# Attention and two feed-forward layers: factors, sums, squares and the mean square take other places in the order

## The chip, the cores and the metric

The kernel runs on one core of a Trainium2 chip. The metric is device microseconds of that core, the median of several runs. Engines are named as in the profile: PE is TensorE (PEld its weight loads), DVE is VectorE, ACT is ScalarE, POOL is GpSimd, SP is SyncE, which only issues DMAs here.

## The reference

Soft-capped attention over 2 batches of 12 heads (448 tokens, head size 64), then a gated feed-forward layer behind an RMS norm, then a second one with a PReLU:

```python
scores = cap * np.tanh(scale * q @ k.T / cap)
attn = np.exp(scores - max); attn = attn / (attn.sum(-1) + 1e-9)
x = (attn @ v)                      # to 896 tokens x 768
xn = x / np.sqrt(np.mean(x * x, -1) + 1e-6) * rms_g
x = silu(xn @ w_gate) * (xn @ w_val) @ w_out      # 768 -> 1536 -> 768
h = x @ w_in                                      # 768 -> 2048
return (np.maximum(h, 0) + alpha * np.minimum(h, 0)) @ w_out2
```

## The kernel before

Heads are worked on in 12 pairs (0 to 11; pairs 0 to 5 are batch 0, 6 to 11 batch 1). The whole order is written by hand. In round `i` of the pair loop TensorE computes the scores of pair `i` (`qk_tail`, L219, and `qk`, three tiles of L229), and then for pair `i - 1` the softmax sums (`sums`, L290, with the tail of the values' product, L272) and the values' product (`pv`, L256). ScalarE makes tanh (L240) and exp (L243) of the scores.

VectorE runs through a list of small steps in each round:

- `evac_o(i - 2)` (L320, tile `ee`) copies a finished product out of PSUM.
- `recip`, in odd rounds (L338 to L343, tiles `gf`, `th`, `tl`), turns the softmax sums of a couple of pairs into factors, cuts them in a high and a low part, and sends both by DMA to `r`. It waits for the DMA that gathers the sums (`gt`, L331).
- `prep(i + 1)` (L195 `hi`, L196 `lo`) cuts the next pair's q and k in two parts.
- `w_bits` (L122, tile `wt`) makes a weight of the feed-forward layer from its packed form: the "remainder" of the title. `w_next` behind it issues the load of another packed weight on SP's queue.
- `evac_u(i - 1)` (L328, tile `us`) copies the softmax sums out of PSUM and issues the two small `gt` DMAs.

In even rounds from 4 on, `norms` spreads the factors of an earlier couple over the partitions on TensorE (L373, `rps`), and VectorE multiplies (L377, `xf`). GpSimd squares those results (`square`, L353 to L361) and adds up the squares of a batch in one tile (`s_546` for batch 0). It also forms sums and differences of weights (`sum1` to `sum4`, L130 `wt<-wt`).

In round 9 `rms_sum` (L398, `ms`) reduces the squares of batch 0 on TensorE, into the PSUM tile with tag "o". That tag has one buffer: the product of a pair (`oo`), the second factor tile of `norms` and `ms` take it in turn, so that each waits until VectorE has read the one before. VectorE copies `ms` out at L572 (tile `spare`).

Behind the last pair, `sums(last)` takes one PSUM tile of two banks, the softmax sums in one (`us`), the product in the other (`oo`). Then the two layers follow as one long chain of block products (L450, L462, L796, L826), in which hooks with a number and a rank put ScalarE's and VectorE's work behind a product. In the first layer's output product, `osplit` and `osplit_low` (L1059, L672, `xx<-b,xx`) make the high and low parts of each operand; "P6" is one of its seven products.

Of the kernel before, what the change touches and what calls it, by code (L numbers as in the profile page):

```python
# [7 lines left out]
F32 = mybir.dt.float32  # L8
# [9 lines left out]
P = 128  # L18
B, H, S, D = 2, 12, 448, 64
# [38 lines left out]
def attn_moe_kernel(ctx: ExitStack, tc: tile.TileContext, units, qk_in, v, sel, w, gvec, alpha, out):  # L58
    nc = tc.nc
# [188 lines left out]
    def upper(name):  # L248
        return ps_o.tile([P, 512], F32, tag="o", name=name)
# [27 lines left out]
    def sums(i):  # L277

        t = pt[i]
        if i == last:  # L280
            both = ps_s.tile([P, 2, 512], F32, tag="s", name="us")
            us[i], oo[i] = both[:, 0], both[:, 1]
        else:
            us[i] = under()
            if i:
                oo[i] = upper("oo")

        def add(h, x, k, m=slice(0, P), src=None):
            q = h + 2 * x
            nc.tensor.matmul(  # L290
                us[i][q * Q:q * Q + Q, HALF[0]], ones[m, :Q], t[m, k, src or HALF[x]], start=k == 2 * TG,
                stop=k // 2 == TG - 1, skip_group_check=True,
            )

        pv_tail(i, False)
        for h in range(2):
            for x in range(2):
                if split[i]:
                    add(h, x, 2 * TG, HEAD[x], HALF[h])
                else:  # L300
                    add(h, x, 2 * TG, HEAD[h])
        if i == 0 and split[i]:
            pv_tail(i, True)
        for n in range(2 * TG):
            for x in range(2):
                add(n % 2, x, n)
        if i and split[i]:
            pv_tail(i, True)
# [58 lines left out]
    def under():  # L367
        return ps_r.tile([P, 512], F32, tag="u", name="rps")
# [10 lines left out]
    def norms(i, *to):  # L379
        for fn in (spread, scaled):  # L380
            for j, rps in enumerate(to):
                fn(i + j, rps)
# [9 lines left out]
    ms_of = {}  # L392

    def rms_sum(b, ms):
        ms_of[b] = ms
        parts = s2.pop(b)
        for n, t in enumerate(parts):
            nc.tensor.matmul(ms[:, :S], ones, t, start=n == 0, stop=n == len(parts) - 1)  # L398

    def rms_keep(b):  # L400
        spare[b] = xpool.tile([P, K3, S], F32, tag="B22h", name="spare")
        rstd[b] = spare[b][:, 2]
# [65 lines left out]
    with tc.manual_schedule():  # L468
# [44 lines left out]
        def a(i, fn, *args):  # L513
            first.setdefault(i, []).append((fn, args))

        def z(i, fn, *args):
            second.setdefault(i, []).append((fn, args))

        conv = conv_seq[:]
        for x in ("A12", "A11"):  # L520
            for g in range(2):
# [4 lines left out]
        for i in range(NPAIR):  # L526
            a(i, load_raw, i + 2)
            a(i, load_v, i + 1)
            if i == 1:
                for put, u in zip((a, z), conv[1:RAW]):  # L530
                    put(i, w_load, u)
            steps = [(prep, i + 1)]
            if i % 2 == 1 and i > 2:
                steps.insert(i < 9, (recip, (i - 3) // 2))
            for step in steps:
                a(i, *step)
            if i - 2 in range(len(conv)):
                a(i, w_bits, conv[i - 2])
                if i - 2 < len(conv) - RAW:
                    a(i, w_next, conv[i - 2])  # L540
            if i % 2 == 0 and i > 2:
                for j in range(2):
                    (a if i == 8 else z)(i, square, i - 4 + j)
            if i - 1 in range(len(conv)):
                if i < 5:
                    z(i, w_top, conv[i - 1], nc.vector.tensor_copy)
                else:
                    a(i, w_top, conv[i - 1])
        a(9, rms_root, 0)
        for n, j in ((3, 0), (4, 1), (9, 6)):  # L550
            z(n, w_hi, conv[j], nc.vector.tensor_copy)
            (a if n == 9 else z)(n + (n == 9), w_lo, conv[j])
        a(11, w_hi, conv[7])
        for put, n, fn, g in ((z, 6, sum1, 0), (z, 7, sum1, 1), (z, 7, sum2, 0), (a, 8, sum2, 1), (a, 8, sum3, 0),
                              (z, 8, sum3, 1), (z, 10, sum4, 0)):
            put(n, fn, "g", g)
        z(10, rms_tail, 0)
# [2 lines left out]
        for i in range(NPAIR):  # L560
            pairs = i % 2 == 0 and i > 2
            if i > 2:
                evac_o(i - 2)
            if i:
                home = {1: (ps_r, "u"), 2: (ps_o, "o")}.get(i)
                qk(i, TG, home[0].tile([P, 1, 512], F32, tag=home[1], name="s") if home else third())
            if i == 8:
                norms(i - 4, under(), upper("rps"))
            if i == 9:
                rms_sum(0, upper("ms"))  # L570
                rms_keep(0)
                nc.vector.tensor_copy(rstd[0], ms_of[0][:, :S])  # L572
                ms_of[0] = rstd[0]
            two = lambda: ps_s.tile([P, 2, 512], F32, tag="s", name="s")
            for g in range(TG - 1):
                qk(i, g, two())
                if pairs and i != 8 and g == 0:
                    norms(i - 4, under(), upper("rps"))
                if (i, g) == (1, 0):
                    oo[0] = upper("oo")  # L580
                    pv(0, range(2))
            if i == 0:
                qk(0, TG - 1, third())
                qk(0, TG, two())
            if i == 1:
                pv(0, range(2, TG))
            if i == 10:
                sums(i - 1)
            if i:
                qk(i, TG - 1, third())  # L590
            soft(i)
            for fn, args in first.pop(i, []):
                fn(*args)
            if i and i != 10:
                sums(i - 1)
            if i == 1:
                evac_o(0)
            if i:
                evac_u(i - 1)
                if i > 1:  # L600
                    pv(i - 1)
                del pt[i - 1], hi[i - 1], lo[i - 1], vt[i - 1]
            for fn, args in second.pop(i, []):
                fn(*args)
# [469 lines left out]

        for way, p, js, hi_at, lo_at in (
# [4 lines left out]
        ):  # L1080
            for h, j in enumerate(js):
                do(o0 + hi_at[h], 0.2, osplit, way, p, j, h)
                do(o0 + lo_at[h], 2.2, osplit_low, way, p, j, h)
        for n, *abc in ((-22, 0, 4, 1, 0), (-21, 0, 5, 3, 4), (-20, 0, 1, 3, 1), (-9, 1, 4, 1, 0), (-8, 1, 5, 3, 4),
                        (-7, 1, 1, 3, 1), (4, 2, 0, 1, 0), (7, 2, 0, 3, 0)):
            do(o0 + n, 3.5, o_sum, *abc)
# [261 lines left out]
```

## Time and profile before

| | us |
|---|---|
| median of 3 runs (539.45 to 539.93) | 539.74 |
| the profiled execution's own time | 540.45 |
| its span | 538.7 |
| TensorE busy in the span | 530.2 (98%) |
| VectorE busy | 448.2 (83%) |
| ScalarE busy | 400.6 (74%) |
| GpSimd busy | 112.0 (21%) |

The chain of work that ended last lies on TensorE for 88% of the span. Times in rows are microseconds from the start of the span. A row of the timeline begins with its start and its duration and ends with the idle time of the engine before it, where there was any, and what ended it.

### The profile page before, as it was taken

The numbers are of one execution on the slowest core, as the hardware profiler recorded it, in microseconds if no ns is written. First come the engines' busy times: TensorE is split into PE (matmuls) and PEld (weight loads), VectorE is DVE, ScalarE is ACT, GpSimd is POOL, SyncE is SP. The second block draws the span as 40 slices with busy tenths as digits, with TensorE's granted clock in tenths as the row PEclk, the third lists the DMA queues.
The fourth block names the chain that finished last, engine by engine and source line by source line (L and its number), as shares of the span: only waits on it lengthen the run. The fifth ranks groups of instructions, "written<-read, shape, count | busy, mean of one in ns | idle before, by whom it ended". The sixth has DMA issues, their size and how long they took to land.

```text
span 538.7 us, 8345 instructions
## 1 busy us (share of the span) xinstructions
PE 530.2 (98%) x3322; PEld 451.1 (84%) x3322; DVE 448.2 (83%) x516; ACT 400.6 (74%) x475; POOL 112.0 (21%) x80
## 2 busy tenths in 40 slices
PE   8999999999999999999999999999999999999997
PEld 5554544699999999999998999999999999999996
DVE  5588889798999968689779796869997897998951
ACT  7989989476766665477688776789989996995530
POOL 0023763300066441010013011110210231210000
PEclk9999999999999999999999999999999999999999
DMA  6856520400344426047865759433466789564111
GB/s 214 317 168 230 179 76 11 159 19 2 102 133 175 161 90 219 0 176 250 273 179 101 157 196 308 80 58 125 169 235 225 215 226 205 98 145 111 51 52 51
DMA packets 22343, 80.05 MB, mean 149 GB/s; under 512 B 3744, under 2 KB 6688, under 8 KB 22304
## 3 DMA queue, kind: packets, MB, share of 16 engines
q1 hardware_dynamic: 16378, 65.43, 35.4%
q0 software_dynamic: 5552, 13.70, 13.9%
q8 instruction: 26, 0.43, 0.3%
q10 hardware_dynamic: 374, 0.39, 0.2%
q14 instruction: 13, 0.11, 0.1%
HBM read 62.99 MB, written 2.75 MB: 122 GB/s over the span
## 4 chain that ended last, share of the span: by engine, by line
PE 88%; DVE 5%; ACT 3%; POOL 2%; DMA 1%; issue 1%; DVEq 0%; SPq 0%; ACTq 0%
PE s L450 19%; PE x L450 13%; PE m L450 13%; PE s L826 8%; PE x L826 7%; PE x L796 5%; PE s L796 5%; PE m L826 4%; PE m L796 3%; PE s L229 2%; PE oo L256 2%; PE rps L290 2%; PE s L462 1%; ACT pt L243 1%; DVE wt L122 1%; PE oo L272 1%
## 5 line engine op out<-in xcount | busy, mean ns | idle before, releaser
L143 DVE TENSOR_TENSOR wl<-wt,wh 128x768 fp32r<-128x768 f32 x109 | 111.5, 1024 | 21.2 <-ACT wh L137 20.8
L137 ACT CAST wh<-wt 128x768 fp32r<-128x768 f32 x106 | 87.7, 830 | 39.7 <-PE s L826 9.2
L130 POOL TENSOR_TENSOR wt<-wt 128x768 f32<-128x768 f32 x25 | 58.4, 2341 | 164.7 <-DVE wl L143 75.7
L117 ACT CAST top<-raw 128x768 f16<-128x768 bf16 x64 | 68.9, 1077 | 21.1 <-DMA raw<-w_in 11.6
L122 DVE SCALAR_TENSOR_TENSOR wt<-raw,top 128x768 uint32<-128x768 uint32 x64 | 66.8, 1045 | 1.0 <-ACT top L117 1.0
L450 PE MATMUL s<-xx,wh 128*128 128x448 f32 x264 | 63.6, 365 | 0.0
L672 DVE TENSOR_TENSOR xx<-b,xx 128x896 fp32r<-128x896 f32 (+1 forms) x55 | 62.1, 1135 | 0.0
L450 PEld LDWEIGHTS s<-xx,wh 128*128 128x128 f32 x264 | 49.3, 187 | 4.8 <-issue 0.9
L450 PE MATMUL x<-xx,wh 128*128 128x448 f32 x204 | 49.9, 366 | 0.0
L450 PE MATMUL m<-xx,wh 128*128 128x448 f32 x204 | 49.5, 364 | 0.0
L893 POOL DMA_DIRECT2D wt<-wt x25 | 21.6, 864 | 126.6 <-DVE wt L122 62.0
L240 ACT ACTIVATE pt<-s,cinv 128x896 f32<-128x896 f32 (+1 forms) x48 | 40.8, 910 | 5.0 <-PE s L229 2.4
L450 PEld LDWEIGHTS x<-xx,wh 128*128 128x128 f32 x204 | 38.2, 188 | 3.5 <-issue 0.4
L450 PEld LDWEIGHTS m<-xx,wh 128*128 128x128 f32 x204 | 38.3, 188 | 3.0
L826 PE MATMUL s<-xx,wh 128*128 128x448 f32 x144 | 40.5, 362 | 0.0
L826 PE MATMUL x<-xx,wh 128*128 128x448 f32 x128 | 36.0, 362 | 0.0
L243 ACT ACTIVATE pt<-pt,cap_t 128x3136 f32<-128x3136 f32 (+2 forms) x13 | 35.2, 2711 | 0.4
L450 PE MATMUL s<-xx,wl 128*128 128x448 f32 x132 | 33.8, 364 | 0.0
L796 PE MATMUL s<-xx,wh 128*128 128x448 f32 x108 | 30.4, 362 | 0.0
L826 PEld LDWEIGHTS s<-xx,wh 128*128 128x128 f32 x144 | 27.0, 187 | 2.3
L796 PE MATMUL x<-xx,wh 128*128 128x448 f32 x96 | 27.3, 363 | 0.6 <-DVE xx L672 0.6
L256 PE MATMUL oo<-pt,vt 128*32 128x448 f32 x264 | 27.1, 540 | 0.4 <-ACT pt L243 0.4
(208 smaller groups left out, 1124.7 us busy)
## 6 DMA issues: line engine op xcount, KB each, us to landing
raw<-w_in SPq DMA_DIRECT2D x68, 768.0 KB
wt<-wt POOLq DMA_DIRECT2D x25, 384.0 KB, 5.3
rw<-qk_in SPq DMA_DIRECT2D x11, 480.0 KB
vt<-v_in SPq DMA_DIRECT2D x12, 288.0 KB
lent<-wt POOLq DMA_DIRECT2D x5, 384.0 KB, 7.0
b<-b POOLq DMA_DIRECT2D x4, 448.0 KB, 5.3
out<-P SPq DMA_DIRECT2D x5, 224.0 KB
out<-b SPq DMA_DIRECT2D x2, 448.0 KB
```

Of the source, the lines that this page charges most:

```text
L117: copy(top_of[u].bitcast(F16)[:, 1::2], raw_t[u].bitcast(BF16)[:, 4:4 * n + 4:4])
L122: nc.vector.scalar_tensor_tensor(out=f_t[u].bitcast(U32), in0=raw_t.pop(u).bitcast(U32)[:, 1:2 * n + 1:2], scalar=13, in1=top_of.pop(u), o ...
L130: add(out=t, in0=f_t[a], in1=f_t[b], op=op)
L137: copy(h_t[u], f_t[u].rearrange("p (k m) -> p k m", m=P))
L143: nc.vector.tensor_tensor(out=l_t[u], in0=f_t[u].rearrange("p (k m) -> p k m", m=P), in1=h_t[u], op=ALU.subtract)
L240: nc.scalar.activation(out=part, in_=st.pop((i, g)), func=AF.Tanh, scale=cinv)
L243: nc.scalar.activation(out=t[:, done:to], in_=t[:, done:to], func=AF.Exp, scale=cap_t)
L256: nc.tensor.matmul(oo[i][q * Q:q * Q + Q, :S], vv[:, n, q % 2 * Q:q % 2 * Q + Q], t[:, n, :], start=i == c == 0, stop=i > 0 and c == TG - ...
L450: nc.tensor.matmul(ps[:, r, :S], lhs, rhs, start=first and n == 0, stop=n == len(mm) - 1, skip_group_check=True,)
L672: nc.vector.tensor_tensor(out=out, in0=a, in1=b, op=op)
L796: nc.tensor.matmul(dst[m], wt[:, kk * MB + m, :], x, start=first and u == 0 and kk == 0 and n == 0, stop=u == UO - 1 and kk == 1 and n == ...
L826: nc.tensor.matmul(dst[m], wt[:, kk * MB + m, :], x, start=first and u == kk == i == 0, stop=last and kk == 1 and i == 2, skip_group_check ...
```

## The change

- `recip` comes ahead of `prep` in rounds 3, 5 and 7 too. (Round 7's `prep` is that of pair 8.)
- In rounds 4, 6 and 8 `sums(i - 1)` and `evac_u(i - 1)` are written ahead of `w_bits`. TensorE's order stays; VectorE's copy and SP's two `gt` DMAs come earlier in their queues.
- `sum2` of weight group 0 goes from behind round 7 to behind the squares of round 8 on GpSimd.
- In round 9 `rms_sum` stands behind the first score tile, and the copy out of PSUM (`keep_sum`) behind `w_bits`.
- The last pair's sums and product get a PSUM tile each.
- The first low part of "P6" is made one hook earlier.

```diff
@@ -278,8 +278,7 @@
         t = pt[i]
         if i == last:
-            both = ps_s.tile([P, 2, 512], F32, tag="s", name="us")
-            us[i], oo[i] = both[:, 0], both[:, 1]
+            us[i], oo[i] = (ps_s.tile([P, 2, 512], F32, tag="s", name=x)[:, 0] for x in ("us", "oo"))
         else:
@@ -516,6 +515,7 @@
+        EARLY = (4, 6, 8)
         conv = conv_seq[:]
@@ -531,10 +531,13 @@
             if i % 2 == 1 and i > 2:
-                steps.insert(i < 9, (recip, (i - 3) // 2))
+                steps.insert(0, (recip, (i - 3) // 2))
             for step in steps:
                 a(i, *step)
             if i - 2 in range(len(conv)):
+                if i in EARLY:
+                    a(i, sums, i - 1)
+                    a(i, evac_u, i - 1)
                 a(i, w_bits, conv[i - 2])
@@ -546,12 +549,19 @@
+
+        def keep_sum():
+            rms_keep(0)
+            nc.vector.tensor_copy(rstd[0], ms_of[0][:, :S])
+            ms_of[0] = rstd[0]
+
+        a(9, keep_sum)
         a(9, rms_root, 0)
...
-        for put, n, fn, g in ((z, 6, sum1, 0), (z, 7, sum1, 1), (z, 7, sum2, 0), (a, 8, sum2, 1), (a, 8, sum3, 0),
+        for put, n, fn, g in ((z, 6, sum1, 0), (z, 7, sum1, 1), (a, 8, sum2, 0), (a, 8, sum2, 1), (a, 8, sum3, 0),
@@ -566,16 +576,13 @@
-            if i == 9:
-                rms_sum(0, upper("ms"))
-                rms_keep(0)
-                nc.vector.tensor_copy(rstd[0], ms_of[0][:, :S])
-                ms_of[0] = rstd[0]
             two = lambda: ps_s.tile([P, 2, 512], F32, tag="s", name="s")
             for g in range(TG - 1):
                 qk(i, g, two())
                 if pairs and i != 8 and g == 0:
                     norms(i - 4, under(), upper("rps"))
+                if (i, g) == (9, 0):
+                    rms_sum(0, upper("ms"))
@@ -591,12 +598,13 @@
-            if i and i != 10:
+            if i and i != 10 and i not in EARLY:
                 sums(i - 1)
...
             if i:
-                evac_u(i - 1)
+                if i not in EARLY:
+                    evac_u(i - 1)
@@ -1074,13 +1082,13 @@
-            (2, "P5", (4, 4, 0), (2, 3, 5), (4, 5, 6)), (0, "P6", (5, 5, 0), (5, 6, 8), (8, 8, 9)),
+            (2, "P5", (4, 4, 0), (2, 3, 5), (4, 5, 6)), (0, "P6", (5, 5, 0), (5, 6, 8), (7, 8, 9)),
...
-                do(o0 + lo_at[h], 2.2, osplit_low, way, p, j, h)
+                do(o0 + lo_at[h], 1.5 if (p, h) == ("P6", 0) else 2.2, osplit_low, way, p, j, h)
```

VectorE in round 9, before; the rows run from the copy of pair 7's product to that of pair 8's softmax sums.

```order
L320 COPY ee<-oo 128x448
L572 COPY spare<-ms 128x448
L338 TENSOR_SCALAR gf<-gt,eps_t 64x28
L339 RECIPROCAL gf<-gf 64x28
L342 CAST th<-gf 64x28
L343 TENSOR_TENSOR tl<-gf,th 64x28
L195 CAST hi<-rw 128x832
L196 TENSOR_TENSOR lo<-rw,hi 128x832
L122 SCALAR_TENSOR_TENSOR wt<-raw,top_94 128x768
L328 COPY us<-rps 128x224
```

The same place now:

```order
L319 COPY ee<-oo 128x448
L337 TENSOR_SCALAR gf<-gt,eps_t 64x28
L338 RECIPROCAL gf<-gf 64x28
L341 CAST th<-gf 64x28
L342 TENSOR_TENSOR tl<-gf,th 64x28
L195 CAST hi<-rw 128x832
L196 TENSOR_TENSOR lo<-rw,hi 128x832
L122 SCALAR_TENSOR_TENSOR wt<-raw,top_94 128x768
L555 COPY spare<-ms 128x448
L327 COPY us<-rps 128x224
```

The copy of `ms` went from the second place to the ninth, behind seven steps that have nothing to do with it.

GpSimd in rounds 7 to 10, before; `wt<-wt` are the weights' sums, `sq` and `s_546` the squares of batch 0, `s_1149` that of batch 1.

```order
L130 TENSOR_TENSOR wt<-wt 128x768 x3
L357 TENSOR_TENSOR sq<-xf 128x448
L361 TENSOR_TENSOR s_546<-s_546,sq 128x448
L357 TENSOR_TENSOR sq<-xf 128x448
L361 TENSOR_TENSOR s_546<-s_546,sq 128x448
L130 TENSOR_TENSOR wt<-wt 128x768 x3
L353 TENSOR_TENSOR s_1149<-xf 128x448
```

The same place now:

```order
L130 TENSOR_TENSOR wt<-wt 128x768 x2
L356 TENSOR_TENSOR sq<-xf 128x448
L360 TENSOR_TENSOR s_546<-s_546,sq 128x448
L356 TENSOR_TENSOR sq<-xf 128x448
L360 TENSOR_TENSOR s_546<-s_546,sq 128x448
L130 TENSOR_TENSOR wt<-wt 128x768 x4
L352 TENSOR_TENSOR s_1149<-xf 128x448
```

One weight sum left the place ahead of the last two squares, and four instead of three stand in a row behind them.

TensorE in round 9 now, with the semaphores that each row waits for, from the mean square to the first matmul of `sums(8)`; before, the `ms` row stood ahead of the first score tile, and the rest was the same.

```order
L397 MATMUL ms<-s_546,ones 128x448 [waits DVE_49,Pool_49]
L229 MATMUL s<-hi 128x448 x2
L229 MATMUL s<-hi,lo 128x448 x2
L229 MATMUL s<-lo,hi 128x448 x2
L229 MATMUL s<-hi 128x448 [waits Activation_49]
L229 MATMUL s<-hi 128x448
L229 MATMUL s<-hi,lo 128x448 x2
L229 MATMUL s<-lo,hi 128x448 x2
L272 MATMUL oo<-pt,vt 32x224 [waits DMAHW5_49,DVE_49]
L272 MATMUL oo<-pt,vt 32x224 x3
```

The wait of the L272 row for VectorE is for the copy `spare<-ms`, since `oo` takes the buffer that `ms` had; between the two matmuls lie two score tiles.

## Rows read from the trace of the kernel before

**Rows 1.** Waits of TensorE, whole span: in total, times, longest.

```profile
PE ms L398 <- POOL s L361: 0.9, 1, 0.9
PE x L796 <- DVE xx L672: 0.6, 1, 0.6
PE rps L373 <- DMA r<-tl: 0.6, 1, 0.6
PE us L256 <- DVE us L328: 0.5, 1, 0.5
```

**Rows 2.** Timeline of TensorE, rounds 9 and 10: start, duration, instruction, idle before.

```profile
68.20 0.61 PE L219 MATMUL s<-rw 64*64 64x224 f32 x8
69.76 1.02 PE L398 MATMUL ms<-s,ones 128*128 128x448 f32 x2 [0.95 <-POOL s L361]
...
72.73 0.39 PE L272 MATMUL oo<-pt,vt 64*32 64x224 f32 x4
...
77.18 0.61 PE L219 MATMUL s<-rw 64*64 64x224 f32 x8
```

**Rows 3.** Timeline of VectorE, rounds 8 and 9.

```profile
61.99 1.15 DVE L377 TENSOR_TENSOR xf<-ee,rps 128x448 f32<-128x448 f32 x2 [0.88 <-PE rps L373]
...
68.34 0.63 DVE L320 COPY ee<-oo 128x448 f32<-128x448 f32 x1 [0.34 <-PE oo L256]
70.81 0.62 DVE L572 COPY spare<-ms 128x448 f32<-128x448 f32 x1 [1.85 <-PE ms L398]
...
71.96 1.35 DVE L342 CAST th<-gf 64x28 fp32r<-64x28 f32 x1
73.35 1.76 DVE L343 TENSOR_TENSOR tl<-gf,th 64x28 fp32r<-64x28 f32 x1
75.03 0.58 DVE L195 CAST hi<-rw 128x832 fp32r<-128x832 f32 x1
75.64 1.03 DVE L196 TENSOR_TENSOR lo<-rw,hi 128x832 fp32r<-128x832 f32 x1
76.59 0.95 DVE L122 SCALAR_TENSOR_TENSOR wt<-raw,top 128x768 uint32<-128x768 uint32 x1
```

**Rows 4.** Timeline of GpSimd, rounds 8 and 9.

```profile
63.69 1.28 POOL L357 TENSOR_TENSOR sq<-xf 128x448 f32<-128x448 f32 x1
...
68.57 1.14 POOL L361 TENSOR_TENSOR s<-s,sq 128x448 f32<-128x448 f32 x1
69.66 5.41 POOL L130 TENSOR_TENSOR wt<-wt 128x768 f32<-128x768 f32 x3
```

**Rows 5.** Timeline of TensorE at the first matmuls of P6.

```profile
286.49 0.36 PE L796 MATMUL x<-xx,wh 128*128 128x448 f32 x1
287.48 0.47 PE L796 MATMUL x<-xx,wh 128*128 128x448 f32 x1 [0.63 <-DVE xx L672]
```

**Rows 6.** Chain of work that ended last, in P6: start, length, what.

```profile
289.36 1.21 PE x L796 x6
```

**Rows 7.** Timeline of VectorE ahead of the low parts of P6.

```profile
282.72 0.96 DVE L143 TENSOR_TENSOR wl<-wt,wh 128x768 fp32r<-128x768 f32 x1 [0.82 <-ACT wh L137]
...
286.34 2.09 DVE L672 TENSOR_TENSOR xx<-b,xx 128x896 fp32r<-128x896 f32 x2
```

**Rows 8.** Timeline of TensorE at the start of the span.

```profile
1.06 3.35 PE L473 MATMUL warm<-ones 128*128 128x128 f32 x14 [1.06 <-DVE ones L470]
4.41 0.74 PE L229 MATMUL s<-hi 64*128 64x448 f32 x2
...
6.47 0.37 PE L229 MATMUL s<-hi 64*128 64x448 f32 x2
```

**Rows 9.** Windows at the span's end: length, busy of each engine, granted clock, DMA.

```profile
535.00:536.00 1.00, 0.06 (x1) 0.00 (x0) 0.69 (x2) 0.00 (x0) 0.00 (x0) 1.00 0.61 224
538.00:538.70 0.70, 0.00 (x0) 0.00 (x0) 0.00 (x0) 0.00 (x0) 0.00 (x0) 0.50 0.00 0
```

## The prediction

> **What bounds the kernel now.** TensorE does: it is busy for 98% of the span and carries 88% of the chain that ended last. So I read its waits first. The list [rows 1] names only four of half a microsecond or more, 2.6 us together: the mean square of batch 0 waits 0.9 for GpSimd's squares, a product in P6 waits 0.6 for VectorE's low part, the spread of the factors in round 8 waits 0.6 for their DMA, and the last pair's product waits 0.5 for the copy of the sums. The change goes at all four. They set what can be gained; what the moves can cost must be looked for in the queue that each step was moved in. The place to look closely is round 9, where three engines meet: TensorE's timeline [rows 2], VectorE's [rows 3] and GpSimd's [rows 4]. In rows 3 the reader is to see that `th`, a cast of 28 elements a partition, took 1.35 us and `tl` 1.76 us, while `hi`, a cast of 832 elements, took 0.58 right behind them. `th` ended at 73.31 and `tl` at 75.11. GpSimd ran three weight sums from 69.66 to 75.07, 1.80 each, so that their ends lie at 71.46, 73.27 and 75.07 [rows 4]. Both small steps ended 0.04 behind the end of a sum: each was held until GpSimd's running instruction was done, and one got through between two sums. The copy `spare<-ms`, which reads PSUM, was not held: 0.62 in the middle of a sum [rows 3].
>
> **The factors' wait (round 8).** With `recip` ahead of `prep` in round 7 and the sums' copy ahead of `w_bits` in round 6, the factors leave VectorE a microsecond or more earlier. The wait of 0.6 [rows 1] goes; between 0 and 0.6 is gained, I take 0.5, since the step right behind it also needs VectorE's copy of pair 6. Round 9 then begins at 67.7 instead of 68.20 [rows 2]. The same moves in rounds 3 to 6 touch none of the four waits; `prep` comes a little later, `w_bits` too, and the rounds behind have room for it. I bound that by one step as long as `hi`, 0.58 [rows 3], either way, and take 0.
>
> **Squares and mean square (rounds 8 and 9).** The first spread product, at 61.99 [rows 3], also comes 0.5 earlier; its first half takes 0.6, so the squares can begin at 62.1. Before, GpSimd was still in `sum2` then and began at 63.69. From there to the end of the last addition, 68.57 + 1.14 = 69.71, the squares took 6.0 [rows 4]. Now they end at 68.1. TensorE reaches the mean square behind the first score tile at about 69.1, so the wait of 0.95 goes as well [rows 2]. TensorE would come to `sums(8)` at 72.73 - 0.95 - 0.5 = 71.3.
>
> **The copy of the mean square (round 9).** This is the step that decides. `sums(8)` may not begin before `spare<-ms` has emptied the one buffer of "o". Before, that copy stood ahead of the factors and ended at 71.43, before `sums(8)` at 72.73 [rows 2, 3]. Now it stands behind `gf`, `th`, `tl`, `hi`, `lo` and `w_bits`. And GpSimd has four sums in a row, from 68.1 on: with 1.80 each [rows 4] they would end at 69.9, 71.7, 73.5 and 75.3. VectorE copies pair 7's product at 67.8 to 68.4, and the two first factor steps take 0.5 (from 71.43 to 71.96 in rows 3): `th` stands ready at 69.0, inside the first sum. If it goes as in rows 3, `th` gets through at 69.9 and `tl` at 71.7; `hi` at 73.5, and being 0.5 long it pushes the fourth sum to 74.0 until 75.8; `lo` then ends at 76.8 (0.95 from start to next start), `w_bits` at 77.7, the copy at 78.3. TensorE begins `sums(8)` at 78.3 instead of 72.73: **+5.6**, the two gains above already in it. Should `gf` be held as well, every step moves one sum on, and the end is the same, since four sums hold four steps in either case.
>
> The Trainium skill, "SBUF — State Buffer", "Who interferes with whom", says that a VectorE step with two inputs in SBUF, or a cast in a fast mode, and a GpSimd instruction that reads SBUF fully block each other, the first to start having the lock. The trace agrees: 1.35 and 1.76 for `th` and `tl`. By that rule all four steps are held, which is the forecast.
>
> **The clock behind the stall.** TensorE would idle from 71.3 to 78.3, 7.0 us. No wait in this trace is near that, but the end of the span shows what idleness does: the last matmul ended at 535.06, and in the window from 538.0 the granted clock is 0.50, that is 1.2 GHz instead of 2.4 [rows 9]. It fell after at most 3 us. At the start of the span two equal matmuls take 0.74 at 4.41 and 0.37 at 6.47 [rows 8]: work from 1.06 on had to go on for 3.4 to 5.4 us before the pace doubled. In 4.3 us at half pace 2.1 us are lost. The ends: nothing, if the clock holds, and 77.18 - 72.73 = 4.45 [rows 2], if all of `sums(8)` and `pv(8)` runs at half pace. I take **+2.1**, from the rows at the start.
>
> The Trainium skill, "TensorE: Matmul & The Clock Gate", "What's actually happening", says that the low clock is the default, which activity lifts. Rows 8 and 9 agree; that a gap in the middle of a kernel does it too, no run shows here so far.
>
> **The last pair.** With a tile each, `pv(last)` no longer waits for the copy of the sums: **-0.5** [rows 1]. The first block product behind it takes the buffer of the sums, which that copy frees well before; the second waits for ScalarE's copy as before.
>
> **P6.** The second matmul starts 0.99 behind the first [rows 5], where 0.20 is the pace (1.21 for six) [rows 6]: **-0.8**. The low part moves into 0.82 of idle time [rows 7] from its place at 286.34; the weight's low part there is pushed by some 0.2 and has slack.
>
> **The sum.** +5.6 + 2.1 - 0.5 - 0.8 = +6.4. Behind round 9 nothing takes it back: TensorE has no long wait from there to P6, and none after it, so that a delay runs through. The profiled execution took 540.45 (span 538.7), 0.7 above the median; on its own time the sum gives 546.9, on the median of 539.74 it gives **546.1**.
>
> **The rivals.**
> - *Held, but the clock stays.* The stall of 7.0 is there, the pace behind it is full: 539.74 + 5.6 - 1.3 = 544.0. For it: no window inside the span shows a lower clock. Against it: the fall at the end came within 3 us [rows 9].
> - *Only the small steps are held.* `th` and `tl` get through at 69.9 and 71.7; `hi`, `lo`, `w_bits` and the copy then run free for 0.6 + 0.95 + 0.9 + 0.6 and end at 74.8: +2.1, less 1.3, gives 540.5. For it: no row here has `hi` and `lo` beside weight sums. Against it: nothing in rows 3 says that length helps.
> - *Nothing is held* (the other side). Then VectorE is through with `th` and `tl` by 69.5 and with the copy by 72.6: TensorE stalls for 1.3 only, `sums(8)` begins 0.1 earlier than before, and with the 1.3 of the two last edits the time is 538.3, faster. It decides from the point at which `th` ends: before 69.3 this holds, at 69.9 the forecast. Against it: `th` and `tl` in rows 3. The release of `ms` for `sums(8)` would still be waited for.
> - *The change doesn't do what it says*: the squares or the factors still come late. Then TensorE waits there first, but the copy is behind the same four sums; the time is the forecast's or up to 1 above it.
>
> **How the numbers follow.** Forecast, with the late squares in it: 0.61. Held with a full clock: 0.22. Small steps only: 0.07. Nothing held: 0.10. Within 0.2% means 1.1 us about 539.74, some of what a measurement here can tell from no change. Faster by more: the last case, 538.3, 0.09 with its spread; the same: the small-step case and the rest of the last, 0.07; slower: 0.84. The range runs from 543.0, one below the case with a full clock (the bound of 0.58 and the unsure halves of the two gains), to 548.4, the sum with the clock's upper end of 4.45; it leaves out the two cheap cases and little else.
>
> **What would show it.** In the changed profile: a wait of TensorE for `spare` of about 7 us ahead of L272 in round 9; `th`, `tl`, `hi` and `lo` each ending just behind one of GpSimd's four sums; the granted clock below 1.0 in the 4 us behind; no wait for `r<-tl`, for the squares, in the last pair or in P6. I am wrong if `th` ends within 0.3 of its start, or if TensorE goes on at 72 to 73.

## The result, and the profile after

The change makes the kernel slower: 545.74 us (545.44 to 546.28) against 539.68 for the kernel before (four executions, 539.45 to 539.93). The ratio is 1.0114, with a 95% interval of 1.0101 to 1.0127. The profiled execution took 545.68, its span is 543.9 and its mean granted clock 0.994; before it was 540.45 and 538.7.

All four waits of [rows 1] are gone from the list of TensorE's waits. In their place stands one, over six times as long as the longest of them. (A second new one, 0.68 for ScalarE in round 10, costs nothing: that round takes 8.30 against 8.33.) The timeline of TensorE in round 9 shows it. The columns are as in [rows 2], namely start, duration, instruction, and in brackets the idle time before it with what ended that.

```profile
68.18 0.61 PE L219 MATMUL s<-rw 64*64 64x224 f32 x8
...
69.53 1.02 PE L397 MATMUL ms<-s,ones 128*128 128x448 f32 x2
...
71.59 0.37 PE L229 MATMUL s<-lo,hi 64*128 64x448 f32 x2
78.24 0.60 PE L272 MATMUL oo<-pt,vt 64*32 64x224 f32 x4 [6.28 <-DVE spare L555]
...
78.64 2.78 PE L289 MATMUL rps<-pt,ones 64*32 64x224 f32 x28
...
83.98 0.61 PE L219 MATMUL s<-rw 64*64 64x224 f32 x8
```

Before, `sums(8)` (L272) began at 72.73 [rows 2]. Now TensorE is through with the scores at 71.96 and then stands still for 6.28 us, until the copy `spare<-ms` has ended. Behind it `sums(8)` and `pv(8)` take 5.74 (78.24 to 83.98), where they took 4.45 before; the 28 small matmuls of L289 take 2.78, where 1.64 is their usual time.

VectorE in the same stretch (compare [rows 3]):

```profile
68.86 1.30 DVE L337 TENSOR_SCALAR gf<-gt,eps_t 64x28 f32<-64x28 f32 x1
70.19 0.32 DVE L338 RECIPROCAL gf<-gf 64x28 f32<-64x28 f32 x1
70.55 1.40 DVE L341 CAST th<-gf 64x28 fp32r<-64x28 f32 x1
71.98 1.74 DVE L342 TENSOR_TENSOR tl<-gf,th 64x28 fp32r<-64x28 f32 x1
73.65 0.57 DVE L195 CAST hi<-rw 128x832 fp32r<-128x832 f32 x1
74.26 2.52 DVE L196 TENSOR_TENSOR lo<-rw,hi 128x832 fp32r<-128x832 f32 x1
...
77.57 0.61 DVE L555 COPY spare<-ms 128x448 f32<-128x448 f32 x1
```

GpSimd (compare [rows 4]):

```profile
62.45 0.94 POOL L356 TENSOR_TENSOR sq<-xf 128x448 f32<-128x448 f32 x1 [1.36 <-DVE xf L376]
...
66.59 1.74 POOL L360 TENSOR_TENSOR s<-s,sq 128x448 f32<-128x448 f32 x1
68.29 7.61 POOL L130 TENSOR_TENSOR wt<-wt 128x768 f32<-128x768 f32 x4
```

The squares are early, as meant: they run from 62.45 to 68.33, and `ms` starts without a wait at 69.53. But right behind them the four weight sums run without a gap until 75.90. The steps `gf` (1.30), `th` (1.40) and `tl` (1.74) each end just behind one of the first three sums; `lo` (2.52) ends at 76.78, 0.88 behind the last one, having begun at 74.26 and needing 1.03 alone. In the kernel before the four took 0.22, 1.35, 1.76 and 1.03 ([rows 3]; 0.22 is `gf` at 71.36): `gf` came there as a sum ended, and `lo` behind the last sum. Only `hi` got in between two sums, at 73.65; the fourth sum had to wait for it, so that the four took 7.61 in all. The copy that TensorE waits for could only start at 77.57.

The windows of the same stretch, with the length of each, the busy time of PE, PEld, DVE, ACT and POOL, then the granted clock:

```profile
74.00:76.00 2.00, 0.00 (x0) 0.00 (x0) 1.97 (x2) 2.00 (x1) 1.90 (x1) 0.56 0.03 4
76.00:78.00 2.00, 0.00 (x0) 0.00 (x0) 2.00 (x3) 1.52 (x2) 0.00 (x0) 0.50 0.00 0
...
80.00:81.00 1.00, 1.00 (x16) 0.51 (x12) 0.00 (x0) 0.19 (x1) 0.00 (x0) 0.50 0.00 0
81.00:82.00 1.00, 1.00 (x20) 0.50 (x16) 0.50 (x2) 0.00 (x0) 0.00 (x0) 0.97 0.00 0
```

The clock is 1.00 until 74, and 0.56 on average from 74 to 76. So it stood at full speed for 0.24 of these 2 us (0.24 x 1.0 + 1.76 x 0.5 = 1.12) and fell at 74.24, 2.28 us behind the last matmul. It is 0.97 from 81 to 82, so it rose at 81.06, 2.8 us after TensorE had work again.

Behind round 9 the two last edits give back what they were to give. The last pair takes 0.71 less than before: from the spread of its factors (L372) to the first block product (L449) it is 99.78 to 104.63, where it was 93.01 to 98.57. In P6 the second matmul follows the first without a wait (compare [rows 5]; the two are one row now):

```profile
292.61 0.57 PE L804 MATMUL x<-xx,wh 128*128 128x448 f32 x2
293.01 0.36 PE L804 MATMUL x<-xx,wl 128*128 128x448 f32 x1
```

The row of 292.61 stood at 286.49 before, 6.12 earlier, and that of 293.01 at 287.79, 5.22 earlier: P6 gives 0.90. The end comes 5.2 us later than before: 6.8 later when round 10 begins (83.98 against 77.18), less 0.7 for the last pair and less 0.9 for P6.

### The profile page after: what moved, and what is told of

It is laid out like the page before. It is cut to its first block, busy times and chain, and to the rows that moved or that the text cites. A ratio compares the mean times of both kernels' runs of the same rounds, so it can differ in the third digit from the quotient of the medians.

```text
span 543.9 us, 8347 instructions
## 1 busy us (share of the span) xinstructions
PE 531.4 (98%) x3322; PEld 451.5 (83%) x3322; DVE 449.7 (83%) x516; ACT 401.4 (74%) x475; POOL 112.1 (21%) x80
## 4 chain that ended last, share of the span: by engine, by line
PE 94%; ACT 2%; DVE 2%; issue 1%; DMA 1%; DVEq 0%
PE s L449 19%; PE m L449 13%; PE x L449 13%; PE s L834 8%; PE x L834 7%; PE s L804 6%; PE x L804 5%; PE oo L256 4%; PE m L834 4%; PE s L229 3%; PE rps L289 3%; PE m L804 3%; PE oo L272 2%; PE s L461 1%; ACT pt L243 1%; ACT pt L240 1%
## 5 line engine op out<-in xcount | busy, mean ns | idle before, releaser
L449 PE MATMUL s<-xx,wh 128*128 128x448 f32 x264 | 63.6, 365 | 0.0
L449 PEld LDWEIGHTS s<-xx,wh 128*128 128x128 f32 x264 | 49.3, 187 | 4.8 <-issue 0.9
L449 PE MATMUL x<-xx,wh 128*128 128x448 f32 x204 | 49.9, 366 | 0.0
L449 PE MATMUL m<-xx,wh 128*128 128x448 f32 x204 | 49.6, 364 | 0.0
L449 PEld LDWEIGHTS x<-xx,wh 128*128 128x128 f32 x204 | 38.2, 187 | 3.5 <-issue 0.4
L449 PEld LDWEIGHTS m<-xx,wh 128*128 128x128 f32 x204 | 38.2, 187 | 3.2 <-issue 0.2
L834 PE MATMUL x<-xx,wh 128*128 128x448 f32 x128 | 36.3, 364 | 0.0
L449 PE MATMUL s<-xx,wl 128*128 128x448 f32 x132 | 33.8, 364 | 0.0
L256 PE MATMUL oo<-pt,vt 128*32 128x448 f32 x288 | 29.5, 540 | 0.6 <-ACT pt L243 0.6
L680 DVE TENSOR_TENSOR b<-s,b 128x896 f32<-128x896 f32 x15 | 16.4, 1090 | 13.3 <-PE s L449 8.1
```

The source lines that it names most:

```text
L256: nc.tensor.matmul(oo[i][q * Q:q * Q + Q, :S], vv[:, n, q % 2 * Q:q % 2 * Q + Q], t[:, n, :], start=i == c == 0, stop=i > 0 and c == TG - ...
L449: nc.tensor.matmul(ps[:, r, :S], lhs, rhs, start=first and n == 0, stop=n == len(mm) - 1, skip_group_check=True,)
L680: nc.vector.tensor_tensor(out=out, in0=a, in1=b, op=op)
L834: nc.tensor.matmul(dst[m], wt[:, kk * MB + m, :], x, start=first and u == kk == i == 0, stop=last and kk == 1 and i == 2, skip_group_check ...
```

## The experiments

The theory: the copy `spare<-ms` stands behind four steps of VectorE, each of which is held until one of GpSimd's sums ends; the clock falls in the stall; the other parts of the change are small gains. The rivals: the queue of eight steps is too long by itself; the restart is slow for another reason than the clock; the fourth sum or the early squares are to blame.

### The copy back to the first place

```diff
-        a(9, keep_sum)
+        first[9].insert(0, (keep_sum, ()))
```

> The changed kernel with one step put back: the copy of the mean square out of PSUM (spare<-ms) stands first in VectorE's row of round 9, ahead of the factors; the four sums of GpSimd and all other parts of the change stay. Theory (the copy's place behind held steps makes the stall): sums(8) begins at about 71.5 to 72, the wait of 6.28 goes to under 1, no window shows the clock below 1.0 there. The factors stay held by the four sums, so that ee(8) comes at about 79 and TensorE waits 1 to 2 us at rps in round 10; round 10 begins at about 76, and the time is 538 to 540, some 6 to 7 below the changed kernel. Rival (the stall comes of the squares or of the score tiles and not of the copy's place): the wait of about 6 us stays, 545.7.

Measured: 539.04 us, ratio to the kernel before 0.999 (0.9977 to 1.0002). TensorE's timeline:

```profile
71.48 0.39 PE L272 MATMUL oo<-pt,vt 64*32 64x224 f32 x4
...
77.92 0.47 PE L372 MATMUL rps<-r,sel_t 64*128 64x448 f32 x1 [0.49 <-DVE us L327]
78.92 0.47 PE L372 MATMUL rps<-r,sel_t 64*128 64x448 f32 x1 [0.53 <-DVE ee L319]
```

`sums(8)` starts at 71.48, without a wait for the copy. One line moved within VectorE's list is worth 6.7 us against the changed kernel. The held steps have not gone: `th` still takes 1.40 and `tl` 1.77, and the steps behind them, `us` and `ee`, come so late that TensorE waits 0.49 and 0.53 for them in round 10. Four of the ten executions took 540.1 to 540.7, at a mean granted clock of 0.996 or 0.997, the other six, with the profiled one, 538.8 to 539.1. The run with the fourth sum alone, below, has the same two waits, and a profile in which the clock falls behind them.

### The sums elsewhere, the copy where the change put it

```diff
-        for put, n, fn, g in ((z, 6, sum1, 0), (z, 7, sum1, 1), (a, 8, sum2, 0), (a, 8, sum2, 1), (a, 8, sum3, 0),
-                              (z, 8, sum3, 1), (z, 10, sum4, 0)):
+        for put, n, fn, g in ((z, 6, sum1, 0), (z, 7, sum1, 1), (z, 10, sum2, 0), (z, 10, sum2, 1), (z, 10, sum3, 0),
+                              (z, 10, sum3, 1), (z, 10, sum4, 0)):
```

> The changed kernel with the order of VectorE kept (the copy still ninth, behind th, tl, hi, lo and w_bits) and GpSimd's four weight sums moved from round 8 to the end of round 10, behind the squares there. Theory (the steps were held by the sums): th and tl take under 0.3 each, lo about 1.0, spare<-ms ends at about 72.6, TensorE waits under 1 us ahead of sums(8), the clock stays 1.0, and the time is about 538.8 (537.5 to 540). Rival (the queue of eight steps ahead of the copy is long by itself): the wait stays near 6 us and the time near 545.7; with half of the held time it would be near 542.

Measured: 542.53 us, ratio 1.0040 (1.0024 to 1.0056). VectorE's timeline, then TensorE's and GpSimd's:

```profile
69.67 0.17 DVE L341 CAST th<-gf 64x28 fp32r<-64x28 f32 x1
...
72.40 0.62 DVE L555 COPY spare<-ms 128x448 f32<-128x448 f32 x1
...
88.30 1.77 DVE L337 TENSOR_SCALAR gf<-gt,eps_t 64x28 f32<-64x28 f32 x1
...
91.90 1.77 DVE L342 TENSOR_TENSOR tl<-gf,th 64x28 fp32r<-64x28 f32 x1
```

```profile
73.08 0.39 PE L272 MATMUL oo<-pt,vt 64*32 64x224 f32 x4 [0.90 <-DVE spare L555]
...
95.54 0.44 PE L372 MATMUL s<-r,sel_t 64*128 64x448 f32 x1 [2.15 <-DMA r<-tl]
```

```profile
83.89 9.74 POOL L130 TENSOR_TENSOR wt<-wt 128x768 f32<-128x768 f32 x5
```

In round 9 it is as the theory says: `th` takes 0.17, the copy, still ninth in the row, starts at 72.40, and TensorE waits 0.90 in place of 6.28. The length of the queue alone is not the cause. But the time was expected at 538.8 and came out 3.7 higher. The five sums that now stand in a row behind the squares of round 10, from 83.89 to 93.63, meet the factors of the last couple: `gf` takes 1.77 there and `tl` 1.77, ending at 93.67, and TensorE waits 2.15 for `r<-tl` and then 0.85 for `xx` (L427), which stands behind `tl` in VectorE's row. The same mechanism, moved by 20 us.

### Both edits together

The diffs of the two experiments above, in one kernel.

> Both edits together: the copy of the mean square first in VectorE's row of round 9, and GpSimd's four sums behind the squares of round 10. Theory: no wait ahead of sums(8), factors free as well, none of the four waits of the kernel before: about 536.5 to 537.5, faster than the kernel before by 2.2 to 3.2 and than either edit alone by 1 to 2. Rival (the sums now stand in the way somewhere behind, in rounds 10 to 12): a new wait of TensorE there, and 538 to 540.

Measured: 541.61 us, ratio 1.0030 (1.0020 to 1.0040). This is the rival, and the time is even above its 538 to 540: with the copy first, the wait for `r<-tl` in round 11 is still 2.12, and here the granted clock also fell to 0.50 behind it (windows from 96 to 98), which it did not in the profile of the run above.

### TensorE kept at work in the stall

```diff
+            if i == 9:
+                fill = under()
+                for _ in range(22):
+                    nc.tensor.matmul(fill[:, :P], ones, ones, start=True, stop=True)
```

First with 44 of these matmuls:

> The changed kernel with 44 added matmuls of ones by ones (128x128, the kind that runs at the span's start; their result is not used) on TensorE ahead of sums(8), so that it is busy in most of the stall; its wait for the copy stays. At the start 14 of them took 3.36 at 1.2 GHz, so 44 should take 5.3 at 2.4 GHz, from 71.96 to about 77.3. Theory (1.3 us behind the stall are lost to the clock): sums(8) still begins at 78.2, the granted clock stays 1.0 from 72 to 84, sums(8) and pv(8) take 4.45 instead of 5.74, and the time is about 544.4. Rival (the slow restart has another reason, such as a cold pipeline or late operands): the clock stays up but the stretch still takes 5.7, and the time stays at 545.7.

Measured: 547.58 us, ratio 1.0142 (1.0125 to 1.0160). This one missed its aim: the 44 are 88 in the trace and took 10.09, so that `sums(8)` began at 81.80 instead of 78.24. It still answers the question: with the clock up, the stretch to round 10 took 4.54 (81.80 to 86.34). Then with half as many:

> As e4_warm with 22 added matmuls in place of 44 (their result is not used): the 44 took 10.09 us at 2.4 GHz and ran over the stall, so 22 take 5.05, from 71.8 to 76.8, and end before the copy does. Theory (the loss behind the stall is the clock's): sums(8) begins at about 78.2 with the granted clock at 1.0 from 72 to 84, sums(8) and pv(8) take 4.5 as in e4_warm, and the time is about 544.5 (544.0 to 545.0). Rival (the filler only moves the loss, since the copy or the sums come later because of it): 545.5 or more.

Measured: 544.51 us, ratio 1.0086 (1.0072 to 1.0100). TensorE's timeline, and one of its windows:

```profile
72.00 5.18 PE L604 MATMUL rps<-ones 128*128 128x128 f32 x44
78.37 0.39 PE L272 MATMUL oo<-pt,vt 64*32 64x224 f32 x4 [1.19 <-DVE spare L555]
...
82.82 0.61 PE L219 MATMUL s<-rw 64*64 64x224 f32 x8
```

```profile
76.00:78.00 2.00, 1.17 (x11) 0.98 (x9) 2.00 (x3) 1.63 (x2) 0.02 (x1) 1.00 0.00 0
```

The wait for the copy is there as before (`sums(8)` starts at 78.37), but the granted clock stays at 1.00, and `sums(8)` and `pv(8)` take 4.45, as in the kernel before. The time is 1.23 below the changed kernel's, and the stretch is 1.29 shorter: with the clock up, nothing of the slow restart is left.

### The last pair's tiles and P6 alone

```diff
-            both = ps_s.tile([P, 2, 512], F32, tag="s", name="us")
-            us[i], oo[i] = both[:, 0], both[:, 1]
+            us[i], oo[i] = (ps_s.tile([P, 2, 512], F32, tag="s", name=x)[:, 0] for x in ("us", "oo"))
...
-            (2, "P5", (4, 4, 0), (2, 3, 5), (4, 5, 6)), (0, "P6", (5, 5, 0), (5, 6, 8), (8, 8, 9)),
+            (2, "P5", (4, 4, 0), (2, 3, 5), (4, 5, 6)), (0, "P6", (5, 5, 0), (5, 6, 8), (7, 8, 9)),
...
-                do(o0 + lo_at[h], 2.2, osplit_low, way, p, j, h)
+                do(o0 + lo_at[h], 1.5 if (p, h) == ("P6", 0) else 2.2, osplit_low, way, p, j, h)
```

> The kernel before with only two parts of the change: a tile each for the last pair's product and sums, and the low parts of P6 due earlier. Theory (the two gains add and nothing in round 9 is needed for them): TensorE's waits us<-us at L256 (0.5) and x<-xx in P6 (0.6) are gone, -0.7 and -0.9, 538.1 (537.6 to 538.7). Rival (VectorE has no room for the earlier low part, a wait shows up in a neighbour of P6): 539 to 540.

Measured: 538.89 us, ratio 0.9986 (0.9977 to 0.9995). The time is 0.2 above the range expected. Both waits are gone, none took their place, and the profiled span is 1.5 shorter than before (537.2). The medians give only 0.84, with an interval of 0.3 to 1.2. So the gain is real, and by the medians smaller than the 1.6 that the one profile pair adds up to; the profiled execution of before was itself 0.7 above its median.

### The mean square's copy alone

The kernel before with `rms_sum` behind the first score tile and the copy behind `w_bits`; the factors, the sums and the rest stay as they were.

```diff
+        def keep_sum():
+            rms_keep(0)
+            nc.vector.tensor_copy(rstd[0], ms_of[0][:, :S])
+            ms_of[0] = rstd[0]
+
+        a(9, keep_sum)
...
-            if i == 9:
-                rms_sum(0, upper("ms"))
-                rms_keep(0)
-                nc.vector.tensor_copy(rstd[0], ms_of[0][:, :S])
-                ms_of[0] = rstd[0]
...
+                if (i, g) == (9, 0):
+                    rms_sum(0, upper("ms"))
```

> The kernel before with only one part of the change: the mean square behind the first score tile and its copy behind w_bits. The squares stay late and three weight sums stand in a row behind them, as before. Theory (the copy's place decides, and three sums hold three of the steps): the factors are ready at 69.6, inside the first sum (69.7 to 71.5); th gets through at 71.5, tl at 73.3, hi behind it, lo behind the third sum at 75.1 to 75.7 and done 0.95 later, the copy at about 78.0; sums(8) begins at 78 instead of 72.73, the clock falls, and the time is about 546 (545 to 547). Rival (the fourth sum or the early squares are needed for the stall): sums(8) begins at 74 to 76, and the time is 541 to 544.

Measured: 547.16 us, ratio 1.0140 (1.0126 to 1.0154). From the waits of TensorE, and VectorE's timeline:

```profile
PE oo L272 <- DVE spare L552: 5.9, 1, 5.9
```

```profile
70.38 1.25 DVE L338 TENSOR_SCALAR gf<-gt,eps_t 64x28 f32<-64x28 f32 x1 [1.16 <-DMA gt<-us]
...
75.72 1.03 DVE L196 TENSOR_TENSOR lo<-rw,hi 128x832 fp32r<-128x832 f32 x1
```

`sums(8)` starts at 78.20, and the time is just above the range expected. This part alone makes the whole loss, and a little more than the whole change, which has the gains beside it. Three sums do for it: here `gf` waits until 70.38 for its DMA and meets the first of them, `th` (1.39) and `tl` (1.74) meet the other two, and `lo` runs free behind them; the copy starts at 77.53, against 77.57 in the changed kernel.

### The factors alone

```diff
+        EARLY = (4, 6, 8)
...
-                steps.insert(i < 9, (recip, (i - 3) // 2))
+                steps.insert(0, (recip, (i - 3) // 2))
...
+                if i in EARLY:
+                    a(i, sums, i - 1)
+                    a(i, evac_u, i - 1)
...
-            if i and i != 10:
+            if i and i != 10 and i not in EARLY:
...
-                evac_u(i - 1)
+                if i not in EARLY:
+                    evac_u(i - 1)
```

> The kernel before with only the factors' moves: recip ahead of prep in rounds 3 to 7, and the sums' copy ahead of w_bits in rounds 4, 6 and 8. Theory: the wait rps<-r of 0.6 in round 8 goes, round 9 begins 0.4 earlier (less up to 0.4 that round 4 loses where recip waits for the sums' transfer); then the mean square waits for GpSimd, whose queue is as before, so it waits longer by what was gained: 539.7 (539.2 to 540.2). Rival (the gain goes through): 539.2 and an unchanged wait at ms.

Measured: 539.19 us, ratio 0.9987 (0.9978 to 0.9996), that is 0.5 faster; I had expected nothing. TensorE, and the sums on GpSimd ahead of the squares:

```profile
68.90 1.02 PE L398 MATMUL ms<-s,ones 128*128 128x448 f32 x2 [0.61 <-POOL s L361]
...
76.32 0.61 PE L219 MATMUL s<-rw 64*64 64x224 f32 x8
```

```profile
59.25 3.64 POOL L130 TENSOR_TENSOR wt<-wt 128x768 f32<-128x768 f32 x2 [3.32 <-DVE wt L122]
```

The wait for the squares did not grow, it shrank from 0.95 to 0.61. I had taken GpSimd's queue as unmoved; but the two sums at its head wait for `w_bits`, and that comes 0.85 earlier (58.22 in place of 59.07), chiefly since `gf` ahead of it no longer waits 0.79 for its DMA. They start at 59.25 in place of 60.09, and the squares behind them at 62.85 in place of 63.69.

### The fourth sum alone

```diff
-        for put, n, fn, g in ((z, 6, sum1, 0), (z, 7, sum1, 1), (z, 7, sum2, 0), (a, 8, sum2, 1), (a, 8, sum3, 0),
+        for put, n, fn, g in ((z, 6, sum1, 0), (z, 7, sum1, 1), (a, 8, sum2, 0), (a, 8, sum2, 1), (a, 8, sum3, 0),
```

> The kernel before with only one part of the change: one weight sum of GpSimd from ahead of the last two squares to behind them, so that four stand in a row there. The factors still come late and the mean square's copy is still ahead of the factors. Theory: the squares end about 1.2 earlier, the wait of 0.9 at ms goes, round 9 is shorter by it; the four sums end at about 75.7, lo ends at about 76.6 as before, so that rps in round 10 waits about 1.0 in two pieces and nothing of the gain is left: 539.4 to 540.0. Rival (the gain goes through): 538.6 to 539.0.

Measured: 542.27 us, ratio 1.0038 (1.0025 to 1.0052), two microseconds above what was expected. The profiled execution was one of 540.26, though, and shows the two waits that the theory names:

```profile
78.36 0.46 PE L373 MATMUL rps<-r,sel_t 64*128 64x448 f32 x1 [0.50 <-DVE us L328]
79.36 0.47 PE L373 MATMUL rps<-r,sel_t 64*128 64x448 f32 x1 [0.54 <-DVE ee L320]
...
86.00 0.61 PE L219 MATMUL s<-rw 64*64 64x224 f32 x8
```

The five executions lay in two groups, 540.3 and 540.9, and 542.3 to 542.6, the latter with a mean granted clock of 0.997. So the same kernel was profiled once more.

> The same kernel as e8_sum2_alone, for a second profile. Of its five executions two took 540.3 and 540.9, and three 542.3 to 542.6 with a mean granted clock of 0.997; the profiled one was of the first kind and shows no stall over 0.6. Theory (a stall that this profile doesn't have lowers the clock in the others): an execution near 542.4 shows one wait of TensorE of over 2 us and about 3 us at a granted clock of 0.50 behind it. Rival (it was that chip's or that moment's): 540.3 and the same four short waits in rounds 8 to 11.

Measured: 541.52 us in a single execution, clock 0.997. TensorE's timeline, and its windows:

```profile
78.28 0.46 PE L373 MATMUL rps<-r,sel_t 64*128 64x448 f32 x1 [0.49 <-DVE us L328]
79.27 0.47 PE L373 MATMUL rps<-r,sel_t 64*128 64x448 f32 x1 [0.54 <-DVE ee L320]
...
87.24 0.61 PE L219 MATMUL s<-rw 64*64 64x224 f32 x8
```

```profile
79.50:80.00 0.50, 0.50 (x7) 0.44 (x5) 0.47 (x2) 0.49 (x2) 0.17 (x1) 1.00 0.01 2
80.00:80.50 0.50, 0.49 (x3) 0.03 (x1) 0.50 (x2) 0.50 (x2) 0.50 (x1) 0.54 0.08 17
80.50:82.50 2.00, 2.00 (x28) 0.82 (x32) 1.97 (x2) 1.62 (x2) 1.92 (x3) 0.50 0.48 144
...
83.00:83.50 0.50, 0.50 (x12) 0.32 (x8) 0.50 (x1) 0.00 (x0) 0.50 (x1) 0.54 0.12 33
83.50:84.00 0.50, 0.50 (x16) 0.12 (x4) 0.50 (x1) 0.00 (x0) 0.38 (x1) 1.00 0.00 0
```

Between these two profiles the clock makes the difference, but not by a longer stall. There is no wait of 2 us; the waits are the same two of half a microsecond. Here the clock fell at 80.0, just behind them, and rose at 83.5, and round 10 took 11.04 (76.20 to 87.24) in place of 9.72 (76.28 to 86.00). That is 1.3; an execution of 542.3 to 542.6 lies another 0.8 to 1.1 above, and where that goes is open, since none was profiled. So two short waits close together can cost more in clock than in waiting, in one execution and not in the next. What decides between them no run shows.

### Two sums here, two there

```diff
-        a(9, keep_sum)
+        first[9].insert(0, (keep_sum, ()))
...
-        for put, n, fn, g in ((z, 6, sum1, 0), (z, 7, sum1, 1), (a, 8, sum2, 0), (a, 8, sum2, 1), (a, 8, sum3, 0),
-                              (z, 8, sum3, 1), (z, 10, sum4, 0)):
+        for put, n, fn, g in ((z, 6, sum1, 0), (z, 7, sum1, 1), (a, 8, sum2, 0), (a, 8, sum2, 1), (z, 10, sum3, 0),
+                              (z, 10, sum3, 1), (z, 10, sum4, 0)):
```

> The changed kernel with the copy of the mean square first in VectorE's row of round 9, two weight sums of GpSimd (instead of four) behind the squares of round 8, and the other two with the one that stands behind the squares of round 10. Theory (each sum in a row holds one step, so two hold only gf and th or one of them, and three in round 10 end at about 89.7, early enough for the last factors): ee(8) at about 76, no waits at rps in round 10, none in round 11 for r<-tl, 537.6 to 538.4. Rival (three sums in round 10 hold the last factors too long): a wait for r<-tl of over 0.5 at about 93, and 538.6 or more.

Measured: 538.11 us, ratio 0.9971 (0.9961 to 0.9982). VectorE's timeline:

```profile
70.63 0.82 DVE L337 TENSOR_SCALAR gf<-gt,eps_t 64x28 f32<-64x28 f32 x1
...
71.84 0.17 DVE L341 CAST th<-gf 64x28 fp32r<-64x28 f32 x1
...
86.64 1.76 DVE L337 TENSOR_SCALAR gf<-gt,eps_t 64x28 f32<-64x28 f32 x1
```

Now a single step is held at each of the two places, `gf`, by 0.6 and by 1.5, and nobody waits for it: TensorE has none of the waits of [rows 1]. A wait of 0.7 stands in round 10, which is as long with it as before (8.30 against 8.33). This kernel is faster than the kernel before and than the change.

And with one place more set back:

```diff
-                steps.insert(0, (recip, (i - 3) // 2))
+                steps.insert(i == 3, (recip, (i - 3) // 2))
```

> As e9_two_and_three, with recip behind prep again in round 3 alone (as in the kernel before). In the changed kernel's profile recip there waited 1.86 for the sums' transfer and ee(2) came late, so that round 4 lost 0.36; in the profile of e9_two_and_three round 4 lost nothing (31.57 to 38.88). Theory (the loss comes and goes with the arrival of that transfer): the same time as e9_two_and_three or up to 0.3 less, 537.8 to 538.2. Rival (recip ahead of prep is needed there too): 538.3 or more.

Measured: 537.81 us, ratio 0.9962 (0.9949 to 0.9974), the best of all; not to be told from the run above by these intervals. It concerns a small loss that the forecast had put at zero. With `recip` ahead of `prep` in round 3, round 4 took 7.66 in the changed kernel, 7.94 with the sums later, but 7.31 with the copy first and with two and three sums, against 7.30 before; with the old place it took 7.31. Where it was lost, `gf` had waited 1.86 and 2.09 for its DMA in round 3, where it was not, 1.34 and 1.42. Since the run above had lost nothing there, this one has no loss to take away.

## Why the prediction was right

The forecast was 546.1, the time is 545.74. Term by term, on the profiled executions:

| step | forecast | after |
|---|---|---|
| `sums(8)` begins | 78.3, +5.6 | 78.24, +5.5 |
| clock behind the stall | +2.1 | +1.3 (5.74 against 4.45) |
| last pair | -0.5 | -0.7 |
| P6 | -0.8 | -0.9 |
| sum | +6.4 | +5.2 |

- **The copy of the mean square.** The place, the cause and the size were right. It was even the case named as "should `gf` be held as well": four steps for four sums, and the end the same. That `hi` slips in and pushes the fourth sum by half a microsecond was right too (7.61 for four sums, against 7.21 where the copy stands first and `hi` comes behind them). The rivals "nothing is held" and "only the small steps" fall with `th`, 1.40, and `lo`, 2.52 long. That the sums hold them, and not the queue's length, is shown by the run with the sums moved (`th` 0.17); that the copy's place makes the loss, by the run with the copy put back (-6.7) and the one with the copy alone (+7.4).
- **The Trainium skill's rule on the shared ports** ("SBUF — State Buffer", "Who interferes with whom"). The runs agree: a step with two inputs in SBUF or a cast is held until the sum ends. It also names the form of `gf`, an operation of a tensor with a scalar, and `gf` was held: 1.30, 1.77 and 1.76 against 0.22. `RECIPROCAL`, which the section doesn't name, took 0.32 in the middle of a sum, as it does alone.
- **The clock.** The step was right and its size was not. I took the 4.3 us that the span's start needs until its matmuls are fast [rows 8]; behind the stall it was 2.8, and the loss 1.29 in place of 2.1. That start was one case of several: in the profile with 44 added matmuls the same first pair took 0.47 at 4.41, where it had taken 0.74. The rival "held, but the clock stays", 544.0, is what the run with 22 added matmuls makes: 544.51.
- **The small gains.** The factors' wait went, and round 8 became 0.37 shorter; I had taken 0.5. The early rounds, put at 0 with a bound of 0.58 either way, lost 0.36 in round 4 in this execution and got 0.26 back in round 5 (7.01 against 7.27). Round 9 began at 68.18 and not at 67.7, which cost nothing, since TensorE then waited for the copy in either case. The last pair gave 0.7 in place of 0.5.
- **The sum.** On its own time the forecast was 546.9, and the profiled execution took 545.68: 1.2 less, of which the clock makes 0.8 and the last two edits 0.3. On the medians forecast and result lie only 0.4 apart, since the profiled execution of before was 0.7 above its median and that of after lies on it. That much of the agreement is luck. Two slips change nothing: the terms of the range's upper end give 548.5 and not 548.4, and the list of waits also has 1.1 at the start of the span, which [rows 1] leaves out and the change does not touch.

The rival "only the small steps" was priced for want of a row with `lo` beside weight sums. The trace of the kernel before has one, two rounds earlier, which speaks against that rival: `lo` began inside a sum, took 2.54 and ended 0.88 behind it, as it does in the changed kernel (GpSimd's row, then VectorE's).

```profile
54.27 2.19 POOL L130 TENSOR_TENSOR wt<-wt 128x768 f32<-128x768 f32 x1
...
54.80 2.54 DVE L196 TENSOR_TENSOR lo<-rw,hi 128x832 fp32r<-128x832 f32 x1
```

The parts add up as well: the copy alone +7.4, the factors alone -0.5, the tiles and P6 -0.8, together +6.1, and the whole change cost 6.06. The fourth sum, which alone costs up to 2.4, is not needed for this account: the run with the copy alone has three sums in the row and the same stall, to 78.20, though `gf` comes later there; early factors with three sums were not run.

## What to carry to other kernels

Before a short step is put behind others, ask what those others share with an engine that runs beside them: here a copy that takes 0.6 us came 6.8 us later than before, 5.2 of them because four steps ahead of it each had to wait for a GpSimd instruction of 1.8 us (77.57 against 72.40 with the sums moved), and it held the one buffer that TensorE needed. Long instructions of GpSimd in a row belong where VectorE has nothing urgent that they can hold; moved as a block, they only met the next urgent steps here, and split in two and three, with the copy first, they cost nothing. And a stall of TensorE is to be priced with what the clock takes behind it, here 1.3 us on top of 6.3.

## What the runs showed of the hardware

- The granted clock fell to 0.50 while TensorE stood still, 2.28 us behind the last matmul, and rose 2.8 us after the restart, within the run of small matmuls.
- It fell to 0.50 for 3.4 us also where TensorE had stood still for no longer than 0.54 at a time, twice within 1.5 us; in another execution of the same kernel with the same two waits it stayed at 1.00. That cost 1.3 us of one round. Behind one wait of 2.12 it fell as well (both edits together), behind one of 2.15 it did not (the sums elsewhere).
- A step of 28 elements a partition, alone 0.17 to 0.22 us, took up to 1.93 beside GpSimd sums (`gf` in round 7 with the factors alone), while a reciprocal of the same size, and a copy out of PSUM, went through beside them in their usual time.
